# Loading the first four of eight input slices for TensorE, and the other four by transposing transfers

## The chip, the cores and the metric

One core of one Trainium2 chip runs the kernel. The metric is the device time of one execution in microseconds (us). TensorE (PE) does the matrix products, ScalarE (ACT) and VectorE (DVE) work on their results, and SyncE (SP) and ACT hand transfers to the DMA engines; "SPq" and "ACTq" in the profile are those two queues of issues.

## The reference

```python
B, S, Dm, Df = 1, 2048, 1024, 3584          # all bfloat16

def reference(x, w_gate, w_up, w_down):
    g = jnp.einsum("bsd,df->bsf", x, w_gate)
    u = jnp.einsum("bsd,df->bsf", x, w_up)
    h = _gelu(g) * u                        # tanh form of gelu
    return jnp.einsum("bsf,fd->bsd", h, w_down)
```

## The kernel before

The 2048 rows of x are worked in two halves of 1024, and a half in two chunks of 512 rows. For the first two products, TensorE needs x with its 1024 columns on the partitions: eight slices `xT[c][ko]` of 128 x 512 per chunk c, one for each block ko of 128 columns. The 3584 columns of the gate and up weights come in eight groups of 3, 3, 3, 3, 4, 4, 4, 4 blocks of 128 columns; three buffers each, `wg0..2` and `wu0..2`, hold the groups in turn (`wload`, line 89, one transfer of 768 or 1024 KB each). A `pair` is one block of 128 columns on one chunk: eight products over ko with gate weights into one PSUM bank, eight with up weights into another, then five operations of ACT and DVE that make a slice of h. After a half's pairs come the products with `w_down` (line 287) and the stores.

In the first half the order is: group 0 on chunk 0, group 1 on chunk 0, group 2 on chunk 0, then all groups on what is left. Group 0 on chunk 0 is special (`first_group`): its six banks are filled side by side, ko by ko, so that work can begin when the first slices are there. A step of ko is six products of 128 x 512.

How chunk 0's slices get onto the partitions is what the change touches. `xpart` (line 172) loads columns of x as they lie, into the tiles `xn`, and `turn(ko)` makes a slice of it: four transposes of 128 x 128 on TensorE into a PSUM bank (line 216), and a copy by DVE (line 222). `xload` (line 98) instead lets the transfer transpose: one issue for a slice, straight into `xT`. `NTURN` is the number of slices that go the first way; it is 6, so slices 6 and 7 of chunk 0, and all eight of chunk 1, come by `xload`.

The first group's weights come in parts (`wpart`, line 178): parts of one ko (96 KB) for ko 0 and 1, and of two (192 KB) from there. SP and ACT share the issues of the start; ACT has six, all before its first arithmetic on group 0's result. After `first_group`'s weights SP issues slices 6 and 7, then gate and up weights of group 1 and of group 2, then the eight slices of chunk 1.

Each queue issues in the order of the program. The framework deals eight completion semaphores out to the transfers in turn, and a transfer whose semaphore is held by an earlier one waits at the head of its queue until that one has landed. So the ninth transfer waits for the first, the tenth for the second, and so on; the queue behind it waits as well. In the built program the first eight are, in that order: x slice 0, up 0, gate 1 (SP), gate 0 (ACT), x slices 2 and 3 (SP), x slice 1 (ACT), up 2-3 (SP), up 1 (ACT).

Of the kernel before, what the change touches and what calls it, by code (L numbers as in the profile page):

```python
# [14 lines left out]
def kernel(  # L15
# [11 lines left out]
    nc = tc.nc  # L27
# [8 lines left out]
    S, Dm = x2.shape  # L36
    Df = w_gate.shape[1]
    NKB = Dm // P
# [14 lines left out]
    NST = 4  # L53
    WDF = 4
    NWARM = 6
    NTURN = 6
    TPC = SCH // P

    pool = ctx.enter_context(tc.tile_pool(name="sb", bufs=1))
# [5 lines left out]
    wg_ring = [pool.tile([P, NKB, GMAX * P], bf16, name=f"wg{r}") for r in range(NW)]  # L65
    wu_ring = [pool.tile([P, NKB, GMAX * P], bf16, name=f"wu{r}") for r in range(NW)]
# [6 lines left out]
    ident = pool.tile([P, P], bf16, name="ident")  # L73
    xn = [pool.tile([P, TPC, 2 * P], bf16, name=f"xn{q}") for q in range(NTURN // 2)]
    banks = [psum.tile([P, 512], f32, name=f"bank{b}") for b in range(8)]
# [9 lines left out]
    def wload(eng, ring, w, g, n, ko=None):  # L85
        c0, cw = STARTS[g] * P, GROUPS[g] * P
        t = ring[n % NW]
        if ko is None:
            eng.dma_start(  # L89
                out=t[:, :, :cw],  # L90
                in_=w[:, c0 : c0 + cw].rearrange("(ko ki) f -> ki ko f", ki=P),
            )
        else:
            eng.dma_start(out=t[:, ko, :cw], in_=w[ko * P : (ko + 1) * P, c0 : c0 + cw])

    def xload(half, c, ko):
        s0 = half * HS + c * SCH
        nc.sync.dma_start_transpose(  # L98
            out=xT[c][ko], in_=x2[s0 : s0 + SCH, ko * P : (ko + 1) * P]
        )  # L100

    def mm1(ps, w, j, c, ko):
        nc.tensor.matmul(  # L103
            ps,
            lhsT=w[:, ko, j * P : (j + 1) * P],
            rhs=xT[c][ko],
            start=(ko == 0),
            stop=(ko == NKB - 1),
        )
# [61 lines left out]
    def xpart(eng, ko, n):  # L171
        eng.dma_start(  # L172
            out=xn[ko // 2][:, :, (ko % 2) * P : (ko % 2 + n) * P],
            in_=x2[0:SCH, ko * P : (ko + n) * P].rearrange("(t p) d -> p t d", p=P),
        )

    def wpart(eng, ring, w, ko, n):
        eng.dma_start(  # L178
            out=ring[0][:, ko : ko + n, : GROUPS[0] * P],
            in_=w[ko * P : (ko + n) * P, : GROUPS[0] * P].rearrange("(ko ki) f -> ki ko f", ki=P),  # L180
        )

    S, A = nc.sync, nc.scalar
    G, U = (wg_ring, w_gate), (wu_ring, w_up)
    xpart(S, 0, 1)
# [5 lines left out]
    xpart(S, 2, 2)  # L193
    wpart(A, *G, 2, 2)
    wpart(S, *U, 2, 2)
    xpart(A, 4, 2)
    wpart(S, *G, 4, 2)
    wpart(S, *U, 4, 2)
    wpart(S, *G, 6, 2)
    wpart(S, *U, 6, 2)  # L200
    for ko in range(NTURN, NKB):
        xload(0, 0, ko)
    for n in (1, 2):
        wload(nc.sync, wg_ring, w_gate, n, n)
        wload(nc.sync, wu_ring, w_up, n, n)
    for ko in range(NKB):
        xload(0, 1, ko)

    def turn(ko):


        tp = [banks[6 + ko % 2].bitcast(bf16)] * 2
        if ko == 0:
            tp = [banks[6].bitcast(bf16), banks[7].bitcast(bf16)]
        for t in range(TPC):
            nc.tensor.transpose(  # L216
                tp[t // (TPC // 2)][:, t * P : (t + 1) * P],
                xn[ko // 2][:, t, (ko % 2) * P : (ko % 2 + 1) * P],
                ident,
            )  # L220
        if ko:
            nc.vector.tensor_copy(out=xT[0][ko], in_=tp[0][:, :SCH])  # L222
        else:
            h = SCH // 2
            nc.vector.tensor_copy(out=xT[0][ko][:, :h], in_=tp[0][:, :h])  # L225
            nc.vector.tensor_copy(out=xT[0][ko][:, h:], in_=tp[1][:, h:SCH])
# [9 lines left out]
    def first_group():  # L236
# [5 lines left out]
        for ko in range(NKB):  # L242
            for j in range(GROUPS[0]):
                mm1(ps[j][0], wg, j, 0, ko)
                mm1(ps[j][1], wu, j, 0, ko)
                if j == (1 if ko == 0 else 0) and ko + 1 < NTURN:
                    turn(ko + 1)
# [48 lines left out]
    for half in range(NHALF):  # L296
# [23 lines left out]
        for ss in range(HS // P):  # L320
            for dc in range(NDC):
# [8 lines left out]
                if xnext:  # L330
                    c, ko = xnext.pop(0)
# [31 lines left out]
```

## Time and profile before

| | us |
|---|---|
| median of three runs | 591.38 (591.13 to 594.27) |
| the profiled execution, its whole time | 591.74 |
| its span, first to last instruction | 590.0 |
| TensorE busy | 582.8 |
| VectorE busy | 244.1 |
| ScalarE busy | 147.8 |

The span is what the rows of the profile add up to; 1.74 us of the profiled execution lie outside it. Times of single instructions count from the span's start. TensorE's granted clock is 1.000 throughout. The first slice of 14.75 us of the DMA engines is nine tenths busy and moves 214 GB/s, the second 237 GB/s.

A transfer has two times: that of its issue on the queue, and that from the start of its issue to its landing, when its semaphore is raised. A group's products can only start when the last weight transfer that they read has landed.

### The profile page before, as it was taken

What the parts mean: (1) busy time and instruction counts of PE and PEld (TensorE: products, weight loads), DVE (VectorE), ACT (ScalarE), POOL (GpSimd) and SP (SyncE); (2) the same over time, 40 slices, a digit from 0 to 9 for tenths busy, and PEclk for the clock granted to TensorE, in tenths of its full rate; (3) what the DMA queues carried; (4) which work ended last, traced back from release to release, by engine and by line L of the source; (5) the groups of instructions that cost most, each with busy time, mean ns of one, the idle gap of its engine ahead of it and who ended that gap; (6) DMA issues with size and microseconds to landing.
All of it is one profiled execution on the core that took longest, in us unless ns stands there. A gap on an engine that the chain in (4) does not pass through costs nothing.

```text
span 590.0 us, 6586 instructions
## 1 busy us (share of the span) xinstructions
PE 582.8 (99%) x2723; PEld 268.4 (46%) x2776; DVE 244.1 (41%) x361; ACT 147.8 (25%) x243; POOL 0.7 (0%) x6
## 2 busy tenths in 40 slices
PE   9999999999999999999999999999999999999998
PEld 4444444444444444444444444444444444444445
DVE  1765665565656400000046565566556662000000
ACT  1433333333333200000023333333333331000000
POOL 0000000000000000000000000000000000000000
PEclk9999999999999999999999999999999999999999
DMA  9906926055050311111203034214000000000000
GB/s 214 237 13 183 321 102 214 11 204 178 1 178 1 107 49 42 45 46 36 55 18 108 16 127 143 89 54 131 12 1 1 2 1 9 19 27 19 27 19 27
DMA packets 58285, 45.51 MB, mean 77 GB/s; under 512 B 16784, under 2 KB 54672, under 8 KB 58256
## 3 DMA queue, kind: packets, MB, share of 16 engines
q1 hardware_dynamic: 56640, 44.31, 25.0%
q10 hardware_dynamic: 1616, 0.79, 0.5%
q8 instruction: 21, 0.34, 0.2%
q14 instruction: 8, 0.07, 0.0%
HBM read 37.49 MB, written 4.19 MB: 71 GB/s over the span
## 4 chain that ended last, share of the span: by engine, by line
PE 96%; DMA 2%; SPq 1%; issue 1%; ACT 0%
PE bank L103 63%; PE bank L287 33%; DMA wu<-in_w_up_dram 1%; DMA xn<-in_x_dram 1%; SPq L98 0%; SPq L178 0%; SPq L89 0%; SPq L172 0%; ACT st L279 0%
## 5 line engine op out<-in xcount | busy, mean ns | idle before, releaser
L103 PE MATMUL bank<-xT,wu 128*128 128x512 bf16 x877 | 213.1, 379 | 1.7 <-DMA wu<-in_w_up_dram 0.8
L103 PE MATMUL bank<-xT,wg 128*128 128x512 bf16 x879 | 213.5, 379 | 1.0
L287 PE MATMUL bank<-wd,hT 128*128 128x512 bf16 (+2 forms) x935 | 193.0, 366 | 0.9
L287 PEld LDWEIGHTS <-hT 128*128 128x128 bf16 x952 | 90.9, 98 | 102.9
L103 PEld LDWEIGHTS <-wu 128*128 128x128 bf16 x896 | 87.5, 98 | 106.7 <-DMA wu<-in_w_up_dram 1.8
L103 PEld LDWEIGHTS <-wg 128*128 128x128 bf16 x896 | 87.7, 98 | 105.3 <-DMA wg<-in_w_gate_dram 0.3
L125 ACT ACTIVATE sq<-bank 128x512 f32<-128x512 f32 x112 | 66.7, 596 | 173.1 <-PE bank L103 167.2
L136 DVE TENSOR_TENSOR tt<-sg,bank 128x512 bf16<-128x512 bf16 x112 | 77.0, 687 | 76.0 <-ACT sg L133 75.9
L128 DVE SCALAR_TENSOR_TENSOR wq<-sq,bank 128x512 f32<-128x512 f32 x112 | 76.9, 687 | 65.6 <-ACT sq L125 65.6
L133 ACT ACTIVATE sg<-wq 128x512 bf16<-128x512 f32 x112 | 70.5, 630 | 87.8 <-DVE wq L128 87.8
L281 DVE CAST st<-bank 128x512 bf16<-128x512 f32 (+2 forms) x17 | 11.1, 652 | 178.3 <-PE bank L287 166.9
L139 DVE TENSOR_TENSOR hT<-tt,bank 128x512 bf16<-128x512 bf16 x112 | 77.0, 687 | 12.4 <-DVE tt L136 0.9
L279 ACT CAST st<-bank 128x512 bf16<-128x512 f32 (+1 forms) x17 | 9.6, 566 | 178.1 <-PE bank L287 178.1
L222 DVE COPY xT<-bank 128x512 bf16<-128x512 bf16 x5 | 2.1, 425 | 6.2 <-PE bank L216 6.2
L160 PE MATMUL bank<-const-bfloat16-1.0 128*128 128x512 bf16 (+1 forms) x8 | 3.4, 570 | 0.8 <-PEq L347 0.8
L216 PEld LDWEIGHTS <-xn 128*128 128x128 bf16 x24 | 1.9, 104 | 1.9 <-DMA xn<-in_x_dram 1.1
L216 PE MATMUL bank<-ident,xn 128*128 128x128 bf16 x24 | 2.6, 235 | 0.0
L160 PEld LDWEIGHTS <-const-bfloat16-1.0 128*128 128x128 bf16 x8 | 1.0, 139 | 1.8 <-issue 1.8
L166 ACT ACT_TABLE_LOAD x1 | 1.3, 1283 | 0.7 <-PEq L347 0.7
L225 DVE COPY xT<-bank 128x256 bf16<-128x256 bf16 x1 | 0.3, 292 | 2.6 <-PE bank L216 2.6
L164 DVE MEMSET gate<- 128x256 uint32 x1 | 0.3, 272 | 0.9 <-PEq L347 0.9
masks.py:199 POOL TENSOR_SCALAR_AFFINE_SELECT ident<-ident 128x128 bf16<-128x128 bf16 x1 | 0.3, 292 | 0.1
(7 smaller groups left out, 1.1 us busy)
## 6 DMA issues: line engine op xcount, KB each, us to landing
wg<-in_w_gate_dram SPq DMA_DIRECT2D x8, 1024.0 KB, 5.3
wu<-in_w_up_dram SPq DMA_DIRECT2D x8, 1024.0 KB, 7.4
wd<-in_w_down_dram SPq DMA_DIRECT2D x7, 1024.0 KB, 9.5
wg<-in_w_gate_dram SPq DMA_DIRECT2D x7, 768.0 KB, 4.7
wu<-in_w_up_dram SPq DMA_DIRECT2D x7, 768.0 KB, 6.9
out_dram<-st SPq DMA_DIRECT2D x31, 128.0 KB, 1.7
wu<-in_w_up_dram SPq DMA_DIRECT2D x3, 192.0 KB, 4.2
xT<-in_x_dram SPq DMA_TRANSPOSE x26, 2.6
```

What stands on the lines that cost most here:

```text
L103: nc.tensor.matmul(ps, lhsT=w[:, ko, j * P : (j + 1) * P], rhs=xT[c][ko], start=(ko == 0), stop=(ko == NKB - 1),)
L125: nc.scalar.activation(self.sq, self.g, ACT.Square, scale=GELU_SQRT_C)
L128: nc.vector.scalar_tensor_tensor(out=self.wq, in0=self.sq, scalar=1.0, in1=self.g, op0=ALU.add, op1=ALU.mult)
L133: nc.scalar.activation(self.sg, self.wq, ACT.Sigmoid, scale=GELU_K)
L136: nc.vector.tensor_tensor(out=self.tt, in0=self.sg, in1=self.g, op=ALU.mult)
L139: nc.vector.tensor_tensor(out=self.dst, in0=self.tt, in1=self.u, op=ALU.mult)
L160: nc.tensor.matmul(b[:, :n], lhsT=warm[:, :P], rhs=warm[:, :n], start=True, stop=True)
L216: nc.tensor.transpose(tp[t // (TPC // 2)][:, t * P : (t + 1) * P], xn[ko // 2][:, t, (ko % 2) * P : (ko % 2 + 1) * P], ident,)
L222: nc.vector.tensor_copy(out=xT[0][ko], in_=tp[0][:, :SCH])
L279: nc.scalar.copy(out=st[:, :cw], in_=ps[:, :cw])
L281: nc.vector.tensor_copy(out=st[:, :cw], in_=ps[:, :cw])
L287: nc.tensor.matmul(ps[:, :cw], lhsT=hT[f][:, ss * P : (ss + 1) * P], rhs=wd[f // WDF][:, f % WDF, c0 : c0 + cw], start=(f == 0), stop=(f = ...
```

## The change

`NTURN` falls from 6 to 4: slices 4 to 7 of chunk 0 now all come by `xload`, and the transfer of x columns for slices 4 and 5, with their two `turn`s (eight transposes on TensorE, two copies on DVE), is gone. SP issues its first five transfers as before, then the four transposing ones, then up weights of group 1, gate and up of group 2, and chunk 1's slices. ACT takes the last four weight parts of group 0 (gate 4-5, up 4-5, gate 6-7, up 6-7), which SP had, and the gate weights of group 1, which SP had too.

```diff
-    NTURN = 6
+    NTURN = 4
...
     xpart(S, 2, 2)
     wpart(A, *G, 2, 2)
     wpart(S, *U, 2, 2)
-    xpart(A, 4, 2)
-    wpart(S, *G, 4, 2)
-    wpart(S, *U, 4, 2)
-    wpart(S, *G, 6, 2)
-    wpart(S, *U, 6, 2)
-    for ko in range(NTURN, NKB):
-        xload(0, 0, ko)
-    for n in (1, 2):
-        wload(nc.sync, wg_ring, w_gate, n, n)
-        wload(nc.sync, wu_ring, w_up, n, n)
+    wpart(A, *G, 4, 2)
+    xload(0, 0, 4)
+    wpart(A, *U, 4, 2)
+    xload(0, 0, 5)
+    wpart(A, *G, 6, 2)
+    xload(0, 0, 6)
+    wpart(A, *U, 6, 2)
+    xload(0, 0, 7)
+    wload(A, *G, 1, 1)
+    wload(S, *U, 1, 1)
+    wload(S, *G, 2, 2)
+    wload(S, *U, 2, 2)
     for ko in range(NKB):
         xload(0, 1, ko)
```

In the built program of the changed kernel the waits for a free semaphore are these. On SP: slice 4 waits for up 0, slice 5 for gate 1, slice 6 for x slices 2-3, slice 7 for up 2-3, group 1's up weights for gate 2-3, group 2's gate weights for gate 4-5, its up weights for slice 6. On ACT: gate 4-5 waits for gate 0, up 4-5 for x slice 1, gate 6-7 for up 1, up 6-7 for slice 4, and group 1's gate weights for slice 5.

## The prediction

> **What bounds the kernel now.** I read the page first, then the chain of work that ended last, then the timelines of TensorE and of SP's queue at the start, then windows of DMA rate.
>
> ```profile
> L103 PE MATMUL bank<-xT,wu 128*128 128x512 bf16 x877 | 213.1, 379 | 1.7 <-DMA wu<-in_w_up_dram 0.8
> ```
>
> TensorE is busy 99% of the span, and in this largest pair of groups it idles 1.7 us in all. Nothing in steady state can be won by this change; the chain says where the rest begins (start, length, what):
>
> ```profile
> 10.58 0.58 SPq L89
> 11.20 7.65 DMA wu<-in_w_up_dram
> 18.90 2.55 PE bank L103 x11
> 21.50 10.74 PE bank L103 x49
> ```
>
> From 18.90 us on the chain is TensorE to the end. Before it, it is a transfer: group 1's up weights, issued at 11.20, landed at 18.85. So the time is "start of the first up products of group 1" plus 571.1 us (590.0 - 18.90), and only what moves 18.90 counts.
>
> ```profile
> 10.04 0.38 PE L103 MATMUL bank<-xT,wu 128*128 128x512 bf16 x1
> 10.25 0.39 PE L216 MATMUL bank<-ident,xn 128*128 128x128 bf16 x4
> 10.48 0.81 PE L103 MATMUL bank<-xT,wg 128*128 128x512 bf16 x2
> ...
> 16.74 1.89 PE L103 MATMUL bank<-xT,wg 128*128 128x512 bf16 x8
> 18.90 1.90 PE L103 MATMUL bank<-xT,wu 128*128 128x512 bf16 x8 [0.26 <-DMA wu<-in_w_up_dram]
> ```
>
> A `turn` puts 0.44 us between two products that otherwise start 0.215 apart (11.12, 11.34, 11.56): it costs TensorE 0.22 us. Group 1 starts at 16.74; eight products later, at 18.47, the up products could start, and they start at 18.90: 0.43 us of stall.
>
> SP's queue (the same columns):
>
> ```profile
> 2.73 0.51 SPq L178 DMA_DIRECT2D wu<-in_w_up_dram  x1
> 5.18 0.37 SPq L178 DMA_DIRECT2D wg<-in_w_gate_dram  x1
> ...
> 8.04 2.50 SPq L98 DMA_TRANSPOSE xT<-in_x_dram  x2
> 10.58 0.58 SPq L89 DMA_DIRECT2D wg<-in_w_gate_dram  x1
> 11.20 0.58 SPq L89 DMA_DIRECT2D wu<-in_w_up_dram  x1
> ```
>
> And windows of the start (from:to, length, busy time of PE, PEld, DVE, ACT, POOL, granted clock, DMA share, GB/s):
>
> ```profile
> 2.00:5.00 3.00, 2.68 (x11) 1.08 (x9) 0.51 (x2) 0.21 (x2) 0.00 (x0) 1.00 0.84 208
> 5.00:8.00 3.00, 2.71 (x18) 1.40 (x19) 0.80 (x2) 0.00 (x0) 0.00 (x0) 1.00 1.07 331
> 8.00:10.40 2.40, 2.40 (x18) 1.13 (x16) 0.47 (x2) 0.00 (x0) 0.00 (x0) 1.00 1.01 286
> 10.40:13.40 3.00, 2.95 (x21) 1.57 (x20) 0.85 (x2) 0.00 (x0) 0.00 (x0) 1.00 1.28 149
> 13.40:18.80 5.40, 5.23 (x25) 2.16 (x22) 2.10 (x4) 2.67 (x5) 0.00 (x0) 1.00 1.07 319
> ```
>
> The DMA engines are the bound of the first 19 us: they run at some 320 GB/s, but for the start and for 10.40 to 13.40, when slices 6 and 7 pass through them. There the share is full (1.28) and the rate is 149 GB/s. Against 319 this loses 3.00 x (1 - 149/319) = **1.6 us** for one run of two transposing transfers between ordinary ones.
>
> **The change part by part.** *Two turns less.* 2 x 0.22 = 0.44 us of TensorE before group 1, whose start could come at 16.30. DVE loses two copies of 0.42 us that lay beside products: nothing.
>
> *Bytes.* Until group 1's up weights are in, the engines move 1024 KB of x, 1536 KB of group 0's and 1536 KB of group 1's weights, before and after. Only dead time and order can change when that ends.
>
> *ACT's five issues.* At 0.38 to 0.53 us each (the rows of its six) some 2.3 us; group 1's gate weights can be issued when slice 5 has landed. ACT's first arithmetic is at 15.86, so 5 us of idle ACT hide them. Had slice 5 not landed by then, ACT's squares would stand behind that issue, and after them DVE and the banks; the estimate below puts it near 10. Price: nothing; with the cover gone, the excess over 15.6.
>
> *Earlier first parts.* Gate 4-5 is issued when gate 0 lands (1.17 + 2.5 = 3.65) and not at 5.18. The window 2 to 5 moves 208 GB/s where 331 are to be had; 192 KB at 331 are 0.6 us. A gain of 0 to 0.6; I take 0, since up 6-7 is issued later (9 to 10, when slice 4 has landed; 7.52 before) and can give it back.
>
> *Four transposing transfers.* SP can issue slice 4 at 5.18 (up 0 landed, 1.26 + 3.9), and the others each 1.2 us on, the two issues before taking 2.50: 5.2, 6.4, 7.6, 8.9. Slice 6 before landed at 8.04 + 5.1 = 13.1, 1.4 after the weights that it stood behind (7.52 + 4.2 = 11.7), and slice 7 0.6 after it. Behind up 2-3 (2.73 + 4.9 = 7.65) this makes 9.1 and 9.7 for slices 4 and 5. TensorE, 0.22 sooner from its fifth step on, needs slices 4 to 7 at 11.1, 12.4, 13.7 and 15.0: covered by 2 us each if the run is not broken up. It costs SP nothing that matters: group 1's up weights go out at 10.2 where they went at 11.20.
>
> The price is the dead time. No row shows transposing transfers on one queue beside ordinary ones on the other: in 10.40 to 13.40 all is on SP's queue. Bounds: none lost at all (-1.6 us), as the slices of chunk 1 alone take 2.8 us each to landing, to a loss of 1.6 at every one of the four (6.4, +4.8). Two things speak for more than before: four in place of two, and ACT's weights now lie between them, so that engines change between the two kinds more than once. I take 1.6 for each two, as in the only row: 3.2, **+1.6**.
>
> [...]
>
> [...]
>
> *Group 1's weights side by side.* Before, both are on SP's queue: gate lands at 10.58 + 5.9 = 16.44, just before TensorE wants it, and up 2.4 us later, which gate's eight products (1.73) nearly cover. Now gate goes by ACT, behind up 6-7, and up by SP, behind slices 6 and 7, with group 2's 1536 KB right behind. Issued within a microsecond of each other and equal in size, they share the engines, and both land when up landed before. Bounds: gate first by its full 2.4 us (no cost of order), or together (1.73 us: the cover of gate's products is lost). I take together: nothing in the order favours gate.
>
> **Sum.** Both land at 18.85 + 1.6 = 20.45. Gate's products start 0.05 later (as 18.90 after 18.85), at 20.50, up's at 22.23: 22.23 - 18.90 = **+3.3 us**. The two turns and the old stall of 0.43 are swallowed: TensorE waits anyway. Span 593.3, execution 595.1; the profiled execution is 0.36 above the median, so the forecast on the median is 591.38 + 3.3 = **594.7**. Later work has cover: group 2's up weights landed at 13.56 + 11.1 = 24.7 and are first read some 10 us after 18.90, chunk 1's slices were all there by 31.6 and are wanted near 38.
>
> **The rivals.** *Each slice pays by itself.* SP issues them 1.25 us apart, and weights on ACT's queue fill each gap: three or four runs at 1.6, so +3.2 to +4.8 on the landing, and 4.9 to 6.5 in the end: **597**. For it: ACT has four weight parts to interleave. [...]
>
> *Not slower: the two queues pass each other.* If ordinary transfers on ACT's queue go on while a slice waits, the 1.6 us vanish: gate and up land at 17.25, gate's products start at 17.30, up's at 19.03: +0.1, **591.5**. If besides gate lands first, by 16.25, TensorE never waits: -0.44 - 0.43, 590.5, the floor. It decides where the windows between 6 and 13 us hold 300 GB/s. For it: engines that are fed by two queues have other work. Against: 10.40 to 13.40, where full engines move little.
>
> *One run, one price.* Four slices bunch and lose 1.6 once: both land at 18.85, up starts at 20.63: +1.7, **593.1**. For it: slice 7 cost only 0.6 after slice 6. Against: only two were issued close together then.
>
> *The change doesn't do what it says:* the built program has the order of the diff; no chance given.
>
> **How the numbers follow.** Forecast 0.42 (593.6 to 596), each by itself 0.18, one run 0.25, queues that pass 0.15. My likeliest time is 594.7. The range of 591.4 to 598.0 leaves out the floor's neighbourhood and more than four full prices. Half a per cent, about what a measurement of this kernel can tell from no change, is 3.0 us: slower means above 594.3. That is most of the forecast (0.35), all of the first rival (0.18) and a little of the third (0.02): 0.55. Faster by that much would need 588.4, below the floor: 0.02 for what I overlook. Within: 0.43.
>
> **What would show it.** Right: the windows between 6 and 13 us fall to 150 to 250 GB/s; gate and up of group 1 land within 1 us of each other near 20; TensorE's idle before line 103 is on gate's weights, about 3 us; 24 transposes become 16. Wrong: gate lands over 2 us before up (order costs nothing), the windows hold 300 (queues pass), or TensorE stalls inside group 0 on a slice or on up 6-7, which I price at nothing: up 6-7 waits for slice 4, and if slice 4 lands after 10 us it comes after 13.9, when it is wanted, and that wait adds to what comes behind only where the DMA engines are not late already.

## The result, and the profile after

| | before | changed |
|---|---|---|
| median of 12 runs, us | 591.64 | 597.63 |
| lowest and highest | 591.13 to 594.27 | 591.93 to 599.72 |
| span of the profiled execution | 590.0 | 594.7 |
| ratio, 95% interval | | 1.0097 (1.0082 to 1.0112) |

The changed kernel is slower by 5.7 us (0.97%). Its runs also lie far apart, 7.8 us where those of before lie within 3.1. The profiled execution took 596.55, 1.1 below the median, so what follows is an execution on the mild side. The granted clock, the share of its full speed that TensorE's clock gets, averages 0.994 to 0.997 in eleven of the twelve runs and 1.000 in the fastest one; in the runs of before beside the experiments it is 0.999 or 1.000.

The gate products as a group of the page before; then, of the changed kernel, the gate and the up products (busy us, mean ns, idle before it) and the ACT transfer among the issues (KB, us to landing):

```profile
L103 PE MATMUL bank<-xT,wg 128*128 128x512 bf16 x879 | 213.5, 379 | 1.0
```

```profile
L103 PE MATMUL bank<-xT,wg 128*128 128x512 bf16 x879 | 215.8, 382 | 4.4 <-DMA wg<-in_w_gate_dram 3.4
L103 PE MATMUL bank<-xT,wu 128*128 128x512 bf16 x877 | 213.5, 380 | 0.9
...
wg<-in_w_gate_dram ACTq DMA_DIRECT2D x1, 768.0 KB, 9.4
```

TensorE now waits on gate weights, 3.4 us of it in one place, and is busy for longer too: 215.8 us for the gate products where it was 213.5. The chain of the changed kernel (start, length, what) and TensorE's timeline at the seam between groups 0 and 1:

```profile
6.12 4.72 DMA xT<-in_x_dram
10.86 9.43 DMA wg<-in_w_gate_dram
20.34 7.69 PE bank L103 x27
```

```profile
16.60 0.38 PE L103 MATMUL bank<-xT,wu 128*128 128x512 bf16 x1
20.34 3.57 PE L103 MATMUL bank<-xT,wg 128*128 128x512 bf16 x8 [3.35 <-DMA wg<-in_w_gate_dram]
23.70 1.95 PE L103 MATMUL bank<-xT,wu 128*128 128x512 bf16 x8
```

The chain runs through slice 5, whose landing at 10.84 lets ACT issue group 1's gate weights at 10.86; they land 9.43 us later. Group 1 starts at 20.34 instead of 16.74. And its first eight gate products take 3.36 us (20.34 to 23.70) instead of 1.73. From the up products on, at 23.70 instead of 18.90, the kernel runs as before: 4.80 later there, 4.7 in the span.

What SP's queue had beside it (issues of line 89 in two narrow windows: duration in ns, start, then the time to landing):

```profile
L89 SPq DMA_DIRECT2D wu<-in_w_up_dram x1: 581/581/581, 10.0 to 10.0; - x1
DMA to landing us min/median/max: 6.1/6.1/6.1
```

```profile
L89 SPq DMA_DIRECT2D wg<-in_w_gate_dram x1: 581/581/581, 10.7 to 10.7; - x1
DMA to landing us min/median/max: 10.3/10.3/10.3
```

Group 1's up weights land at 16.1, 4.2 us before its gate weights, which are wanted first; group 2's gate weights, wanted some 10 us later, land at 20.9, 0.6 us after them. The windows show that the DMA engines were not idle meanwhile, though they moved little in the first of them (DMA share and GB/s stand last):

```profile
10.40:13.40 3.00, 2.95 (x15) 1.35 (x15) 0.00 (x0) 0.00 (x0) 0.00 (x0) 1.00 0.94 200
13.40:18.80 5.40, 3.58 (x17) 1.44 (x15) 2.02 (x4) 2.59 (x5) 0.00 (x0) 1.00 1.07 338
```

And windows around the seam (length, PE busy and count, ..., granted clock, DMA share, GB/s) show the second loss:

```profile
16.90:20.30 3.40, 0.08 (x1) 0.00 (x0) 3.19 (x6) 1.99 (x5) 0.00 (x0) 1.00 1.10 326
20.40:23.80 3.40, 3.40 (x9) 1.20 (x10) 2.21 (x4) 0.30 (x1) 0.00 (x0) 0.50 1.28 269
23.90:27.30 3.40, 3.40 (x18) 1.56 (x16) 1.86 (x3) 1.23 (x2) 0.00 (x0) 1.00 1.22 98
```

After 3.4 us almost without a product the granted clock is 0.50 for 3.4 us: 9 products in that window, 18 in the next of the same length. Of the 4.80 us, 3.17 are gate's late landing (a start of its products at 18.90 - 1.73 = 17.17 would have kept up's start of before) and 1.63 are the slower clock (3.36 - 1.73).

### The profile page after: what moved, and what is told of

It reads as the page before. It is cut to its first block, busy times and chain, and to the rows that moved or that the text cites. A ratio compares the mean times of both kernels' runs of the same rounds, so it can differ in the third digit from the quotient of the medians.

```text
span 594.7 us, 6569 instructions
## 1 busy us (share of the span) xinstructions
PE 585.2 (98%) x2715; PEld 269.0 (45%) x2768; DVE 243.7 (41%) x359; ACT 148.2 (25%) x243; POOL 0.7 (0%) x6
## 4 chain that ended last, share of the span: by engine, by line
PE 96%; DMA 3%; issue 1%; SPq 0%; ACT 0%
PE bank L103 63%; PE bank L290 32%; DMA wg<-in_w_gate_dram 2%; DMA xT<-in_x_dram 1%; DMA wu<-in_w_up_dram 1%; SPq L98 0%; SPq L172 0%; ACT st L282 0%
## 5 line engine op out<-in xcount | busy, mean ns | idle before, releaser
L103 PE MATMUL bank<-xT,wg 128*128 128x512 bf16 x879 | 215.8, 382 | 4.4 <-DMA wg<-in_w_gate_dram 3.4
L103 PE MATMUL bank<-xT,wu 128*128 128x512 bf16 x877 | 213.5, 380 | 0.9
```

The source lines that it names most:

```text
L103: nc.tensor.matmul(ps, lhsT=w[:, ko, j * P : (j + 1) * P], rhs=xT[c][ko], start=(ko == 0), stop=(ko == NKB - 1),)
```

## The experiments

The first four undo two parts of the change by themselves and together, and test the clock.

**1. No transposing slices.** Slices 4 to 7 as they lie, turned on TensorE.

```diff
-    NTURN = 4
+    NTURN = 8
...
-    xload(0, 0, 4)
+    xpart(S, 4, 2)
     wpart(A, *U, 4, 2)
-    xload(0, 0, 5)
     wpart(A, *G, 6, 2)
-    xload(0, 0, 6)
+    xpart(S, 6, 2)
     wpart(A, *U, 6, 2)
-    xload(0, 0, 7)
```

> The changed kernel with slices 4 to 7 loaded as they lie (two transfers of 256 KB on SP) and turned on TensorE; group 1's gate weights still by ACT. Theory (the loss is that gate shares the engines with up and with group 2's gate weights, and then a clock that drops after the idle time): the engines lose no time to transposing slices before 20 us, some 1.9 us less than in the changed kernel, so gate lands near 18.4 instead of 20.3; TensorE idles about 1.3 us ahead of group 1, too short for the clock to drop; about 592.9 us, 1.0 to 1.5 above before. Rival (the transposing slices between ordinary transfers are the loss): gate lands by 16.5, no idle, 591.6, the same as before.

Measured: 595.41 us, ratio 1.0072 (1.0059 to 1.0085). The windows from 7 to 13 us, of this run, of the changed kernel, and of the kernel before:

```profile
7.00:9.00 2.00, 1.92 (x13) 0.90 (x11) 0.85 (x2) 0.00 (x0) 0.00 (x0) 1.00 1.18 298
9.00:11.00 2.00, 2.00 (x14) 1.02 (x13) 0.42 (x1) 0.00 (x0) 0.00 (x0) 1.00 1.10 324
11.00:13.00 2.00, 1.45 (x10) 0.60 (x8) 0.42 (x1) 0.00 (x0) 0.00 (x0) 1.00 1.10 327
```

```profile
7.00:9.00 2.00, 1.96 (x13) 0.90 (x11) 0.68 (x2) 0.00 (x0) 0.00 (x0) 1.00 1.14 243
9.00:11.00 2.00, 2.00 (x14) 1.01 (x13) 0.42 (x1) 0.00 (x0) 0.00 (x0) 1.00 1.19 271
11.00:13.00 2.00, 1.95 (x10) 0.94 (x10) 0.00 (x0) 0.00 (x0) 0.00 (x0) 1.00 0.85 157
```

```profile
7.00:9.00 2.00, 2.00 (x17) 1.06 (x16) 0.43 (x1) 0.00 (x0) 0.00 (x0) 1.00 1.07 312
9.00:11.00 2.00, 1.95 (x15) 1.02 (x14) 0.75 (x2) 0.00 (x0) 0.00 (x0) 1.00 1.29 260
11.00:13.00 2.00, 2.00 (x13) 1.01 (x13) 0.53 (x2) 0.00 (x0) 0.00 (x0) 1.00 1.02 96
```

Without transposing slices the engines hold 298 to 327 GB/s. Against 325 GB/s the changed kernel loses 2 x (82 + 54 + 168)/325 = 1.9 us in these six, and the kernel before 2 x (13 + 65 + 229)/325 = 1.9 as well. The same sum over the other profiles with four slices (runs 2, 3, 5, 6, 8, 9 and 10 and the repeats) gives 1.0 to 1.9: four slices cost the engines no more than two did.

```profile
8.82 11.79 DMA wg<-in_w_gate_dram
```

Gate by ACT landed at 20.6 even so, as late as in the changed kernel (20.3) with no transposing slice ahead of it. That is neither theory's landing, 18.4 or 16.5. The time was a miss for both as well, 2.5 us above the one and 3.8 above the other; TensorE waited 1.40 us inside group 0 besides, and run 4 shows why.

**2. Gate back on SP.** One issue moved; the four transposing slices stay.

```diff
-    wload(A, *G, 1, 1)
+    wload(S, *G, 1, 1)
     wload(S, *U, 1, 1)
```

> The changed kernel with one issue moved: group 1's gate weights on SP's queue ahead of its up weights, as before the change; the four transposing slices stay. Theory (order): gate lands near 16.5 to 17.0, up near 19, TensorE idles under 1.5 us and the clock stays at 1.000; 591.5 to 592.5 us. Rival (transposing slices): the dead time stays, gate and up both late, 594.5 us or more.

Measured: 591.15 us, ratio 0.9993 (0.9983 to 1.0002); gate landed at 15.6, up at 18.2, clock 1.000. TensorE has no stall at the seam:

```profile
16.83 1.89 PE L103 MATMUL bank<-xT,wg 128*128 128x512 bf16 x8
18.55 1.89 PE L103 MATMUL bank<-xT,wu 128*128 128x512 bf16 x8
```

All of the loss is gone with this one line, and the transposing slices are still there. The run was repeated:

> The version that did best, again, for its interval and as the base of the next two: the changed kernel with group 1's gate weights on SP ahead of up. Theory: TensorE is the bound from its first product, the two turns less (0.44 us) and the stall of 0.43 us are gained; 590.9 to 591.3 us, 0.3 to 0.8 below before, at most the 0.87 of the forecast's floor.

Measured: 591.00 us, ratio 0.9992 (0.9983 to 1.0001). Its chain:

```profile
11.52 6.94 DMA wu<-in_w_up_dram
18.51 4.28 PE bank L103 x19
```

Up's products start at 18.51, against 18.90 before: 0.4 of the 0.87 us that the forecast's floor gave. Both medians are 0.6 us below before and both intervals just reach 1, so that it is faster is likely and not settled.

**3. Idle time filled.** 14 products of constants between the groups.

```diff
             first_group()
+            for _ in range(14):
+                dummy(banks[7])
```

> The changed kernel with 14 products of constants (3.0 us at the full clock) on TensorE between group 0 and group 1, in a bank that is overwritten afterwards; no transfer is touched. Theory (the idle time of 3.5 us lets the clock fall to half for 3.4 us, at a price of 1.7 us): the granted clock stays 1.000, group 1's first gate products take 1.73 us and not 3.36; 1.6 to 1.9 us less than the changed kernel, near 595.8. Rival (the clock is no part of it, the landing of gate varies from run to run): the same as the changed kernel, 597.5.

Measured: 596.77 us, ratio 1.0085 (1.0071 to 1.0099). In the profiled execution the clock stayed at 1.000 and the gate products took 1.74 us, but gate landed at 21.4. It was run again with the changed kernel beside it:

> The filled kernel again (14 products of constants between group 0 and group 1 of the changed kernel), beside the changed kernel on the same chip. Theory: clock at 1.000 throughout, below the changed kernel by what the drop costs on average, 0.7 to 1.7 us. Rival (the clock is no part of it): within 0.3 us of the changed kernel.

Measured: 597.10 us, ratio 1.0087 (1.0068 to 1.0107), 0.6 below the changed kernel's 597.66 and well inside both intervals. This time gate landed at 23.1, TensorE idled 3.44 us behind the constants, and the clock fell all the same:

```profile
23.18 3.60 PE L103 MATMUL bank<-xT,wg 128*128 128x512 bf16 x8 [3.44 <-DMA wg<-in_w_gate_dram]
26.57 3.07 PE L103 MATMUL bank<-xT,wu 128*128 128x512 bf16 x7
29.47 1.89 PE L103 MATMUL bank<-xT,wg 128*128 128x512 bf16 x8
```

Here it stayed at half for longer: gate and up products took 3.39 and 2.90 us where 1.73 each are usual, 2.8 us in all. The mean granted clock of the single runs says how often it fell. One stretch of 3.4 us at half in 595 makes 0.997, two make 0.994. It fell in 4 of the 10 filled runs and in 15 of the 18 runs of the changed kernel (result and run 5). So the filling does keep the clock up more often, but by the medians it brought only 0.6 to 0.9 us, and the intervals overlap; what the drop is worth on the median is not settled by it.

**4. Both undone.** Runs 1 and 2 together.

```diff
-    NTURN = 4
+    NTURN = 8
...
-    xload(0, 0, 4)
+    xpart(S, 4, 2)
     wpart(A, *U, 4, 2)
-    xload(0, 0, 5)
     wpart(A, *G, 6, 2)
-    xload(0, 0, 6)
+    xpart(S, 6, 2)
     wpart(A, *U, 6, 2)
-    xload(0, 0, 7)
-    wload(A, *G, 1, 1)
+    wload(S, *G, 1, 1)
```

> Both: slices 4 to 7 loaded as they lie and turned on TensorE, and group 1's gate weights on SP ahead of up; the other weight parts of group 0 still by ACT. Both theories: no stall of a microsecond anywhere; TensorE's products and eight turns set group 1's up products at 18.9 at the earliest, 591.0 to 591.8 us, as before.

Measured: 594.06 us, ratio 1.0045 (1.0033 to 1.0058): a miss. Part of the chain of this kernel, and the product that waited:

```profile
7.24 6.59 DMA wu<-in_w_up_dram
14.27 0.22 PE bank L217 x4
14.49 1.29 PE bank L103 x6
```

```profile
13.88 0.39 PE L103 MATMUL bank<-xT,wu 128*128 128x512 bf16 x1 [1.67 <-DMA wu<-in_w_up_dram]
```

Here a weight part of group 0, up 4-5, takes 6.6 us to land (4.0 in the changed kernel), and TensorE waits for it inside group 0. SP, free of four transposing issues, gave out group 1's gate weights at 5.1 us, and these ran beside group 0's parts on ACT's queue. The transposing issues, 1.2 us each and with waits of their own, had been holding SP's later weights back. So runs 1 and 4 changed two things, and the time says little on transposing; the windows do. (The profiled execution, 595.78, is the longest of the five. At the seam it lost 2.35 us, up's products starting at 21.25, which is what the median shows; the rest of its excess lies behind the last arithmetic.)

**5. The changed kernel again.**

> The changed kernel once more, beside the next runs on the same chip. Theory (order, and a clock that drops after a long idle time): gate of group 1 lands 3 us or more after up, between 20 and 21.5 us; the median 597 to 598. If the idle time ahead of group 1 is over 3.4 us the clock falls to half for about 3.4 us after it; if it does not fall in this execution, the gate products take 1.73 us and the span is at most the gate's landing plus 572.8.

Measured: 597.66 us (593.69 to 599.74), ratio 1.0095 (1.0066 to 1.0124). The profiled execution was the mildest, 593.69: gate landed at 19.1, TensorE idled 2.25 us, the clock did not fall, span 591.9.

```profile
19.18 1.90 PE L103 MATMUL bank<-xT,wg 128*128 128x512 bf16 x8 [2.25 <-DMA wg<-in_w_gate_dram]
```

The expectation had the landing at 20 us or later, 3 us or more after up; here it was earlier, and 2.5 us after up. Span and landing go together: landing + 0.05 + 572.83 (590.0 less 17.17, the latest start of gate's products that keeps the time of before) gives 592.0 here, 594.3 for the 21.43 of run 3 (594.2 measured), and 593.2 for the first profile, whose 1.5 more is the clock.

**6. Queues exchanged.** Group 1's gate by SP, up by ACT.

```diff
-    wload(A, *G, 1, 1)
-    wload(S, *U, 1, 1)
+    wload(A, *U, 1, 1)
+    wload(S, *G, 1, 1)
```

> The changed kernel with group 1's two weight transfers exchanged between the queues: gate by SP behind the transposing slices, up by ACT. Theory (what goes by ACT behind four weight parts lands last, whichever it is): gate lands near 16, up at 20 to 21.5; gate's products start without a stall, up's start when up has landed; the wait is 1.73 us shorter and too short for the clock to drop; 593 to 594.3 us. Rival (gate's size or place, or the transposing slices, make it late): gate is late here too, 596 or more.

Measured: 596.68 us, ratio 1.0088 (1.0075 to 1.0101).

```profile
16.36 1.89 PE L103 MATMUL bank<-xT,wg 128*128 128x512 bf16 x8
21.58 3.56 PE L103 MATMUL bank<-xT,wu 128*128 128x512 bf16 x8 [3.33 <-DMA wu<-in_w_up_dram]
```

The mechanism is as expected: gate by SP lands at 15.9, up by ACT at 21.5. The time is not: the wait was still 3.33 us, and the clock fell (eight up products took 3.35).

**7. The kernel before, all slices turned.** No transposing transfer for chunk 0, weights on the queues of before.

```diff
-    NTURN = 6
+    NTURN = 8
...
     wpart(S, *U, 4, 2)
+    xpart(A, 6, 2)
```

> The kernel before with slices 6 and 7 loaded as they lie by ACT and turned on TensorE, so that no transposing transfer runs before 20 us; the weights' queues and order as before. Theory (transposing slices between ordinary transfers cost the engines about 1.6 us, once, and in the kernel before this was just about covered): windows between 7 and 13 us hold 300 GB/s or more, up of group 1 lands near 17.3 instead of 18.85, and the time does not move because two more turns (0.44 us) take the place of the 0.43 us stall: 591.2 to 592.0, no difference. Rival (turning more slices costs more than it saves, as in the runs without transposing slices that were slower): 593 or more, with a stall inside group 0.

Measured: 592.57 us, ratio 1.0018 (1.0009 to 1.0027), 0.6 above the expected range: no gain, and a small loss. The windows between 7 and 13 us held 313, 309 and 327 GB/s and up landed at 17.35, as expected: up comes 1.5 us sooner without the two slices, so the 1.6 us that the forecast read from the window of before are real. They bring nothing, since TensorE is then the bound: up's products start at 19.34, 0.44 later than before. Group 0 took 0.4 us longer than its two more turns explain; this was not followed up.

**8 and 9. A pause and no late transfer.** In the version of run 2, TensorE is made to wait for GpSimd between the groups (`k` stands for 4 in the one and 9 in the other).

```diff
+    scratch = pool.tile([P, SCH], bf16, name="scratch")
+    nc.gpsimd.memset(scratch, 0.0)
...
             first_group()
+            for i in range(2):
+                nc.tensor.matmul(banks[7], lhsT=warm[:, :P], rhs=scratch, start=True, stop=True)
+                for _ in range(k if i == 0 else 0):
+                    nc.gpsimd.memset(scratch, 0.0)
```

> The version of the run before with a pause put on TensorE between group 0 and group 1 and no transfer touched: a product reads a scratch tile, GpSimd then overwrites the tile 4 times, and a second product waits for that. About 2 us of pause by an estimate from GpSimd's 128x128 memset (0.20 us). Theory (a pause under about 3 us leaves the clock alone): the time grows by the pause and two products, clock 1.000.

> The same with 9 overwrites, a pause of about 4 to 5 us. Theory (a pause of more than some 3.3 us lets the clock fall to half): the granted clock is 0.5 for 3.4 us or more after the pause, and the time grows by the pause and by 1.7 us or more besides. Rival (the clock falls for another reason, with the late transfer): the time grows by the pause alone, clock 1.000.

Measured: 595.27 us (1.0058, 1.0041 to 1.0075) and 598.48 (1.0116, 1.0102 to 1.0130). TensorE's timelines, the short pause and the long one:

```profile
20.03 0.38 PE L306 MATMUL bank<-scratch,const-bfloat16-1.0 128*128 128x512 bf16 x1 [2.38 <-POOL scratch L308]
20.25 1.89 PE L103 MATMUL bank<-xT,wg 128*128 128x512 bf16 x8
21.97 1.89 PE L103 MATMUL bank<-xT,wu 128*128 128x512 bf16 x8
```

```profile
22.35 0.59 PE L306 MATMUL bank<-scratch,const-bfloat16-1.0 128*128 128x512 bf16 x1 [5.29 <-POOL scratch L308]
22.73 3.62 PE L103 MATMUL bank<-xT,wg 128*128 128x512 bf16 x8
26.14 2.05 PE L103 MATMUL bank<-xT,wu 128*128 128x512 bf16 x8
```

After 2.38 us of idle time eight products take 1.72 us, after 5.29 they take 3.41. No transfer was late in either (gate and up had landed by 18.3 us). That a pause of 5.29 us alone halves the clock is shown. The short pause's theory, that the clock is left alone, held in the profile and not in every run: two of its four runs have a mean granted clock of 0.997, and these two are the longer ones, 595.80 and 596.36 us beside 593.62 and 594.74. So its median grew by 4.3 us and its profiled span by 3.4 (592.9 less 589.5). The long pause's windows add where the clock fell:

```profile
16.10:19.60 3.50, 0.96 (x5) 0.33 (x4) 2.96 (x5) 2.42 (x5) 2.25 (x5) 1.00 1.10 326
19.70:22.30 2.60, 0.00 (x0) 0.00 (x0) 2.39 (x5) 0.63 (x1) 2.37 (x5) 0.50 1.12 319
22.40:26.40 4.00, 4.00 (x10) 1.43 (x10) 0.28 (x1) 0.00 (x0) 0.00 (x0) 0.50 0.80 142
```

It was at half before the pause ended, 2.6 us after the last product's end at 17.06 and 3.0 after its start, and stayed there past 26 us.

**10. Group 2 behind gate.** Group 2's weights leave SP's queue.

```diff
     wload(A, *G, 1, 1)
     wload(S, *U, 1, 1)
-    wload(S, *G, 2, 2)
-    wload(S, *U, 2, 2)
+    wload(A, *G, 2, 2)
+    wload(A, *U, 2, 2)
```

> The changed kernel with group 2's two weight transfers moved from SP to ACT, behind group 1's gate; SP has group 1's up, then chunk 1's slices. Theory (gate was late because group 2's gate weights, next on SP's queue, took engine time from it): gate lands with up or soon after, 17.5 to 18.8 us instead of 19.1 to 20.3; TensorE idles 1 to 2 us, the clock holds; 592.5 to 594 us, and steadier. Rival (what goes by ACT behind four parts is slow by itself): gate still near 20, 596 or more.

Measured: 594.61 us (593.08 to 595.57), ratio 1.0049 (1.0035 to 1.0064).

```profile
18.47 1.90 PE L103 MATMUL bank<-xT,wg 128*128 128x512 bf16 x8 [2.43 <-DMA wg<-in_w_gate_dram]
```

Gate landed at 18.4, in the expected range, the clock held in this execution, and by the median about half of the loss is gone: group 2's weights on SP's queue were about half of what the changed kernel lost. The median is 0.6 above the expected range; the profiled execution, 593.08, is the fastest of the five and lies in it, and in three of the other four the clock fell (0.997). The other half is still there: up, by SP, landed at 15.1, 3.3 us before gate. What held gate back then is not shown; chunk 1's transposing slices had moved up to second place on SP's queue, and group 2's gate weights stood behind gate on ACT's. The edit has a side effect too: ACT, held up by its issue of group 2's up weights, began its arithmetic on group 0 at 19.27 instead of 15.94, which cost TensorE some 0.1 us here.

## Why the prediction was right, and where its steps were not

*The bound.* Right. Once the clock is back at full, what follows group 1's first products moves with them: span and start agree within 0.2 us in the profiles of all kernels but run 4's, whose end came 1.7 us later still.

*Range and sign.* 597.63 lies in the range near its upper end; the rise is 5.7 to 6.0 us where 3.3 were forecast. Of the signs named ahead, the idle time on gate's weights (3.35 us, "about 3") and the 16 transposes came; gate and up within 1 us of each other did not (4.2), and the windows held 157 to 271 GB/s. The forecast's start of gate's products, 20.50, is 20.34 in the profile, but that is luck: two wrong terms cancel in it, 1.6 us for more dead time that was not there and the order of the queues taken too lightly. The first rival's time, 597, is nearer than the forecast's, and its reason, a price for every slice, is not what the windows show.

*Four transposing transfers: "1.6 for each two: 3.2, +1.6".* This failed as a size. The run of four lost 1.9 us of engine time in the profile of the changed kernel and 1.0 to 1.9 in the other profiles with four, the run of two before it 1.9: the term is 0 or less, not +1.6, and the price is for the run. That was the third rival's term. The slices landed at 9.9, 10.8, 11.3 and 11.7, each over a microsecond ahead of their use, and up 6-7 at 13.93, in time.

The windows from 11 to 13 us moved 96 GB/s before and 157 in the changed kernel, where slices pass between ordinary transfers, beside 327 in runs 1 and 7, which have none there.

*Group 1's weights side by side: "I take together".* This step failed, and it is the cause. The bounds were "gate first" and "together"; gate came last, 4.2 us after up. I had named group 2's 1536 KB right behind up on SP's queue and then let them count for nothing. Up was done at 16.1, and group 2's gate weights, issued at 10.67, were still on their way until 20.9. That gate's place on ACT's queue is the cause is shown by run 2 with its repeat (order restored, loss gone), run 6 (exchanged, the other one late) and run 1 (no transposing slice ahead, gate as late as in the changed kernel); run 10 shows group 2's weights as about half of it. The other half stays open.

*The clock.* Missing. I priced a stall at its length; 3.4 us of idle time halved the clock for 3.4 us more, 1.6 us in the profiled execution. Run 9 shows the same with no late transfer: after 5.29 us of idle time eight products took 3.41 us. It does not come every time, but in 15 of 18 runs of the changed kernel the mean granted clock is below 1.000, so the median has it in. How much of the median it is stays open, since run 3 and its repeat could not tell.

A shortest pause that lowers the clock is not shown. The limits named in the expectations, 3.4 us for run 5, about 3 for run 8 and some 3.3 for run 9, were my estimates. The clock held after 2.25, 2.38 and 2.43 us of idle time in the profiles of runs 5, 8 and 10, and fell with 3.33 to 5.29 us in those of the changed kernel, of run 3's repeat and of runs 6 and 9; but it also fell in two of run 8's four executions, whose pause is 2.38 us in the profile. In run 9 it fell 2.6 us after the last product's end, and in run 3's repeat 2.4 us after it (0.78 on average from 21 to 23 us: at 1.00 until 22.1, at 0.50 from 22.2, the last constant product's end at 19.74).

*Two turns less, 0.44 us.* Right in kind: hidden under the stall in the changed kernel. In run 2 and its repeat 0.4 of the 0.87 us that the turns and the old stall were worth together show in the profiles, and 0.6 in the medians, where no difference is not excluded.

*ACT's issues.* Right: gate was issued at 10.86, 5 us before ACT's first square.

*Left open.* What made the other half of gate's delay in run 10, why the same kernel's gate lands anywhere from 19.1 to 23.1 us (the latter in the filled one), and why one of its 12 runs took 591.93.

## What to carry to other kernels

When two queues feed the same engines, count as a transfer's rivals all that the other queue holds until it lands, not only its twin: without group 2's weights on SP's queue the time was 594.61 us, where the changed kernel has 597.63. Here it paid to put what is needed first and what is needed next on one queue, in that order (591.15 and 591.00 us in run 2 and its repeat). A step that seems slow, like a transposing issue (1.2 us each here), may be what keeps later transfers from overtaking earlier ones (without those issues run 4's SP gave out group 1's gate weights at 5.1 us), so look at what a faster queue gives out sooner. Price a stall of TensorE at more than its length: here stalls of 3.33 to 3.44 us cost 1.6 to 2.8 us on top, while a pause of about 2.4 us lowered the clock in two of four runs.

## What the runs showed of the hardware that was not expected

A run of four transposing transfers between ordinary ones cost the engines 1.0 to 1.9 us in ten profiles, a run of two 1.9 us in one. With the long pause the granted clock fell while TensorE was still idle (0.50 from 19.70 us, the next product at 22.35). The half-speed time was 3.4 us after 3.35 us of idle time and more than 6 us (19.70 to 26.40) with a pause of 5.29. A transfer of 768 KB by ACT beside a full SP queue took 9.2 to 11.5 us to land in five profiles (the changed kernel's two, run 3's two and run 6's), where group 1's gate weights, first of two on SP's queue behind the transposing slices, took 5.6 to 5.9 in the kernel before and in runs 2, 8 and 9.
